# One-bank score tiles, half-width exponentials and a new order of TensorE's steps in a fused attention and gated-MLP block

## The chip, the cores and the metric

The kernel runs on one core of one Trainium2 chip. The metric is device time in microseconds (us), taken as the median of several executions. One further execution was recorded by the hardware profiler; durations and waits quoted below come from that execution.

## What is computed

The block has 2048 positions of width 512. Its first half is attention with 32 heads of 16 channels, its second a gated MLP that mixes positions. Cut to what matters:

```python
def _A_ref(x, wqkv, wo):
    H = 32; Dh = D // H                       # 16
    qkv = ...(x @ wqkv).reshape(B, S, 3, H, Dh)...
    scores = jnp.einsum("bhqd,bhkd->bhqk", q, k) * Dh ** -0.5
    p = _softmax(scores, axis=-1)
    o = jnp.einsum("bhqk,bhkd->bhqd", p, v)
    return ...o... @ wo
...
h = x + _A_ref(_layernorm(x), A_wqkv, A_wo)
h2 = h + _B_ref(_layernorm(h), B_w_in, B_w_sp, B_b_sp, B_w_out)
```

The change touches only the attention loop, and one line of the stage ahead of it.

## The kernel before, in words

The program has four stages: projections (to about 162 us of the span), the attention loop (to about 1331 us), the first part of the MLP, and the second. Around the change, each engine has its instructions in the order in which the code emits them (`manual_schedule`), and waits at the first one that is not ready.

**The attention loop** works on groups of four heads (`hg`) and blocks of 512 queries (`qb`). A *unit* is one block of 128 keys (`kb`) for four heads and 512 queries. One **iteration** of the loop takes two units, `kb` and `kb1`; there are 256 iterations, eight for each `hg`, `qb`. In an iteration:

- `score` (L777 to L789) makes the scores of two heads, the pair number `p` of a unit. Head `t` = 0 has its operands in rows 0 to 49 of TensorE's array and head `t` = 1 in rows 64 to 113 (`RG` is 64), and products of different `t` start side by side in the trace. Each product fills 512 columns, which is one PSUM bank. A tile `s` holds both products, that is two banks; there are two such tiles (`ps_s`, `bufs=2`). One ScalarE exponential of 1024 columns (L788) moves the tile to `pt` in SBUF.
- `weigh` (L791 to L797), called **the weighing** here, multiplies the four `pt` halves of one unit by V and adds them into the tile `pv` over sixteen units. It is done one unit late: the first weighing of an iteration is that of the previous iteration's `kb1`, the second that of `kb`. At the first iteration of each eight, `gather` (L799) copies the finished `pv` out, half on VectorE (L802) and half on ScalarE (L803); three iterations later `invert` takes a reciprocal of the sums on VectorE.
- `max_pair` (L205 to L253) makes, eleven calls ahead of need, the row maxima that the exponentials subtract. It returns eight **steps**, each a product of 128 queries with 512 keys into one of three one-bank tiles `m0`, `m1`, `m2`, and what reads that bank. Four steps (`four`) belong to `t` = 1. For `t` = 0, two steps take keys 1024 to 2047; and the keys below 1024 are replaced by the sums and differences of its two halves: `minus` is the product with the differences, of which ScalarE takes the absolute value (L233, called **Abs** here), and `plus` the product with the sums, where one VectorE instruction (L237) adds Abs to it and takes the maximum, since max(a, b) = (a + b)/2 + |a - b|/2. The other six steps end in one VectorE maximum each (L228). At the end of every eighth call VectorE reduces all maxima (L243), GpSimd splits them in two, and in the next iteration VectorE transposes them (`max_rows`, L255), from where SyncE's DMAs bring them beside the queries.

PSUM has eight banks: three for `m`, four for `s`, one for `pv`. The last eleven iterations have no steps left; the `m` banks are closed there, and a third tile `s` and a bank `h` take their place. GpSimd meanwhile prepares weights for the MLP, in portions that are handed out per iteration.

The steps are called one by one with a bank number written into the code, `steps.pop(0)(b)`. The emission order of one iteration before is: the scores of `kb` (`p` 0, then 1), `four[0]` (bank 2), keys 1024 to 1535 (bank 0), the first weighing, `minus` (bank 1), the copies of `gather` if due, `four[1]` (bank 2), scores of `kb1` `p` 0, `four[2]` (bank 0), scores of `kb1` `p` 1, `four[3]` (bank 1), `plus` (bank 2), the second weighing, `max_rows` if due, keys 1536 to 2047 (bank 1).

In the projection stage `ahead` (L532) lays the steps of the first eleven calls between projection products, on five banks in turn, in an order of its own.

Of the kernel before, what the change touches and what calls it, by code (L numbers as in the profile page):

```python
# [8 lines left out]
F32 = mybir.dt.float32  # L9
# [4 lines left out]
AF = mybir.ActivationFunctionType  # L14
ALU = mybir.AluOpType
AX = mybir.AxisListType
PSUM = bass.MemoryType.PSUM
DRAM = bass.MemoryType.DRAM

P = 128  # L20
# [7 lines left out]
NB = S // P  # L28
HB = NB // 2
NQ = S // 512  # L30
# [4 lines left out]
KM = 50  # L35
PB = 6
FIRST = 2
RG = 64
# [20 lines left out]
def block_kernel(ctx: ExitStack, tc: tile.TileContext, x, wqkv, wo, w_in, w_sp4, b_sp, w_out, out):  # L59
# [7 lines left out]
    nc = tc.nc  # L67
# [76 lines left out]
    kst = [kpool.tile([RG + KM, 2, S], F16, name="kst0")]  # L144
    uvs = [kpool.tile([KS, 2, 1024], F16, name="uvs0")]
    qst, mx, turned = {}, {}, {}
# [58 lines left out]
    def max_pair(m):  # L205

        g, i = divmod(m, 8)
        hg, qb = divmod(g, NQ)
        q, k, w = qst[g], kst[hg % 2], uvs[hg % 2]
        if i == 0:
            mx[g] = sm.tile([P, 16, 4], F32, name="mx")
            nc.gpsimd.memset(mx[g][:, :8, 3:], LOW)
        c, p = slice(i % 4 * P, i % 4 * P + P), i // 4
        at = lambda t, e: mx[g][:, t * 8 + i, e:e + 1]

        def scores(t, keys, b):  # L220
            r = slice(RG * t, RG * t + KS)
            acc = bank(b)
            nc.tensor.matmul(acc, q[r, p, c], keys[r, p], start=True, stop=True)  # L223
            return acc

        def one(t, e, b):
            acc = scores(t, k[:, :, 512 * e:512 * e + 512], b)
            nc.vector.reduce_max(at(t, e if t else e - 1), acc, axis=AX.X)  # L228

        def minus(b):  # L230
            acc = scores(0, w[:, :, 512:], b)
            ab[0] = sm.tile([P, 512], F32, name="ab")
            nc.scalar.activation(ab[0], acc, AF.Abs)  # L233

        def plus(b):
            acc = scores(0, w[:, :, :512], b)
            nc.vector.tensor_tensor_reduce(ab[0], acc, ab[0], 0.5, LOW, ALU.add, ALU.max, at(0, 0))  # L237

        def last(b):
            one(0, 3, b)  # L240
            if i == 7:
                nm = sm.tile([P, 2, 8], F32, name="nm")
                nc.vector.tensor_reduce(nm.rearrange("p t i -> p (t i)"), mx.pop(g), axis=AX.X,  # L243
                                        op=ALU.max, negate=True)
                parts = sm.tile([P, 2, 2, 8], F16, name="mparts")
                nc.gpsimd.tensor_scalar(nm, nm, 1.0 / ONE, 1.0, op0=ALU.mult, op1=ALU.mult)  # L246
                nc.gpsimd.tensor_copy(parts[:, :, 0], nm)
                nc.gpsimd.tensor_sub(parts[:, :, 1], nm, parts[:, :, 0])
                turned[0] = (g, parts)

        ab = {}
        four = [lambda b, e=e: one(1, e, b) for e in range(4)]
        return [four[0], lambda b: one(0, 2, b), minus, four[1], four[2], four[3], plus, last]  # L253

    def max_rows():  # L255

# [12 lines left out]
    with ExitStack() as pre:  # L269
        p2 = pre.enter_context(tc.tile_pool(name="pre_2", bufs=2))  # L270
        pc = pre.enter_context(tc.tile_pool(name="pre_c", bufs=1))
        pt = pre.enter_context(tc.tile_pool(name="pre_pt", bufs=2, space=PSUM))
# [257 lines left out]
        todo, done = [], [0]  # L530

        def ahead(k):  # L532
            for _ in range(k):
                m = done[0] // 8
                if not todo and m < LEAD:
                    steps = max_pair(m)
                    todo.extend(steps[i] for i in (0, 1, 3, 2, 4, 6, 5, 7))
                if todo:
                    todo.pop(0)(done[0] % 5)
                    done[0] += 1  # L540
# [67 lines left out]
        for g in range(3):  # L608
            a, b = 4 * g, 4 * g + 4
# [123 lines left out]
    def make_h(sb, acc):  # L733

        o2, h = o2s.pop(sb), xrs[sb]
        for d in range(DB):
            mm3(acc, o2[0][:, d, :], o2[1][:, d, :], wo2[0][:, d, :], wo2[1][:, d, :],
                d == 0, d == DB - 1)
        nc.vector.scalar_tensor_tensor(h, acc, h_down, h, op0=ALU.mult, op1=ALU.add)
        nc.sync.dma_start(h_scr[sb * P:(sb + 1) * P, :], h)  # L740
        hst[sb] = e2.tile([P, 6], F32, name="st")
        nc.vector.bn_stats(hst[sb], h)
# [24 lines left out]
    with ExitStack() as at:  # L767
# [2 lines left out]
        uvs.append(kpool1.tile([KS, 2, 1024], F16, name="uvs1"))  # L770
        fixed(kst[1])
        pp = at.enter_context(tc.tile_pool(name="pp", bufs=6))
        ps_s = at.enter_context(tc.tile_pool(name="ps_s", bufs=2, space=PSUM))
        ps_v = at.enter_context(tc.tile_pool(name="ps_v", bufs=1, space=PSUM))
        pv = {}

        def score(hg, qb, kb, p):  # L777

            q, k = qst[hg * NQ + qb], kst[hg % 2]
            turn[0] += len(later)  # L780
            pool = later[0] if turn[0] % 3 == 2 else ps_s
            s = pool.tile([P, 2, 512], F32, name="s")
            for t in range(2):
                r = slice(RG * t, RG * t + KM)
                nc.tensor.matmul(s[:, t, :], k[r, p, kb * P:(kb + 1) * P], q[r, p, :],  # L785
                                 start=True, stop=True)
            t = pp.tile([P, 2, 512], F32, name="pt")
            nc.scalar.activation(t, s, AF.Exp, scale=scales_[hg // 2])  # L788
            return t  # L789

        def weigh(hg, qb, kb, pts):  # L791
            if kb == 0:
                pv[0] = ps_v.tile([P, 512], F32, name="pv")
            for j in range(4):
                c = (4 * kb + j) * VW
                nc.tensor.matmul(pv[0][32 * j:32 * j + 32, :], vst[hg % 2][:, c:c + 32],  # L796
                                 pts[j % 2][:, j // 2, :], start=kb == 0, stop=kb == NB - 1)  # L797

        def gather(hg, qb, pool=sm):  # L799

# [39 lines left out]
        pool = nc.gpsimd  # L840
# [176 lines left out]
                quarters(p, c)  # L1017

        units = [(hg, qb, kb) for hg in range(HG) for qb in range(NQ) for kb in range(NB)]
        prev, turn, later, asked = None, [0], [], []  # L1020
        for n in range(0, len(units), 2):
            (hg, qb, kb), (_, _, kb1) = units[n:n + 2]
            if m % 8 < 7 and n < 480:
                work(4.1 if m % 8 < 6 else 2.0)
            if n == 480:
                work(None)
            if hg + 1 < HG and n % 64 < 24 and n % 4 == 0:
                load_k(hg + 1, [n % 64 // 4])
            if hg + 1 < HG and n % 64 < 12 and n % 4 == 2:
                load_uv(hg + 1, [n % 64 // 4])  # L1030
            if hg + 1 < HG and n % 64 == 30:
                copy_v = load_v(hg + 1)
            if hg + 1 < HG and n % 64 == 36:
                copy_v()
            if kb == 2 and n // NB + 3 < HG * NQ:
                load_q(n // NB + 3)
            steps = max_pair(m) if m < 8 * HG * NQ else []
            m += 1
            if not steps and not later:
                maxima.close()  # L1040
                later.append(attn.enter_context(
                    tc.tile_pool(name="ps_l", bufs=1, space=PSUM, side="right")))
            step = lambda b: steps and steps.pop(0)(b)
            pts = [score(hg, qb, kb, 0), score(hg, qb, kb, 1)]
            step(2)
            step(0)
            if prev is None:

                pv[0] = ps_v.tile([P, 512], F32, name="pv")
                for j in range(4):  # L1050
                    nc.tensor.matmul(pv[0][32 * j:32 * j + 32, :], vst[0][:, :32],
                                     vst[0][:, :512], start=True, stop=True)
            else:
                weigh(*prev)
            step(1)
            if kb == 0 and n:
                gather(*units[n - 1][:2])
            step(2)
            pts1 = [score(hg, qb, kb1, 0)]
            step(0)  # L1060
            pts1.append(score(hg, qb, kb1, 1))
            step(1)
            step(2)
            weigh(hg, qb, kb, pts)
            if turned:
                max_rows()
            step(1)
            prev = (hg, qb, kb1, pts1)
            if kb == 6 and n > NB:
                invert()  # L1070
            if n in (486, 490, 506):
                asked.append(load_o(h_rows[min((n - 486) // 4, 2)]))
            if n in (492, 496, 508):
                asked.pop(0)()
            if n in (494, 502):
                split_o(h_rows[(n - 494) // 8])
            if n in (500, 504):
                sb = h_rows[(n - 500) // 4]
                make_h(sb, later[0].tile([P, 512], F32, name="h"))
                mv, rs = scale_h(sb)  # L1080
                hns[sb] = e2.tile([P, D], F32, name="hn", bufs=3)
                nc.vector.tensor_scalar(hns[sb], xrs.pop(sb), mv[:, 0:1], rs,
                                        op0=ALU.subtract, op1=ALU.mult)
# [305 lines left out]
```

## Time and profile before

| what | us |
|---|---|
| median of 3 runs | 1777.41 |
| their range | 1774.44 to 1777.6 |
| the profiled execution | 1775.32 |
| its span, first to last instruction | 1773.2 |
| TensorE busy in the span | 1736.3 |
| VectorE busy | 1407.9 |
| ScalarE busy | 1271.0 |
| GpSimd busy | 824.3 |

The profile names engines PE (TensorE's products), PEld (its weight loads), DVE (VectorE), ACT (ScalarE), POOL (GpSimd), SP (SyncE). A timeline row gives the start, the time from the start of the first to the end of the last instruction in the row, the engine, the line, what is written and read, and a count; idle time of the engine ahead of it and what ended it stand in brackets. Products overlap in TensorE's pipeline, so the distance between the starts of two rows tells more than the rows' own lengths. The granted TensorE clock was 0.999 over the span.

### The profile page before, as it was taken

How to read it: one execution, taken by the hardware profiler on the slowest of the kernel's cores; microseconds unless marked ns; L12 is line 12 of the kernel's file. 1: busy time of each engine (PE TensorE's matmuls, PEld its weight loads, DVE VectorE, ACT ScalarE, POOL GpSimd, SP SyncE). 2: the span in 40 equal slices, each digit the busy share in tenths (PEclk: the TensorE clock that was granted, in tenths of full speed). 3: DMA queues.
4: the chain of work that ended last, by engine and by line, in shares of the span. 5: the costliest groups of instructions: out<-in, count | busy, mean ns of one | idle time of the engine just before them, and what ended most of it. 6: DMA issues, size and time to landing. Idle time of an engine off the chain costs nothing.

```text
span 1773.2 us, 32918 instructions
## 1 busy us (share of the span) xinstructions
PE 1736.3 (98%) x11621; PEld 661.6 (37%) x11621; DVE 1407.9 (79%) x2896; ACT 1271.0 (72%) x1614; POOL 824.3 (46%) x1088
## 2 busy tenths in 40 slices
PE   9999999999999999999999999999998999999999
PEld 4433222222222222222222222222225666777776
DVE  7688999999999999999999999999925886111112
ACT  4335999999999999999999999999984555011000
POOL 1322677765762168776677757700002775110010
PEclk9999999999999999999999999999999999999999
DMA  5534332232221235435344434300024463753450
GB/s 178 158 102 145 82 83 84 79 91 69 74 62 20 57 110 145 127 112 138 95 123 128 126 102 136 95 21 10 12 65 115 134 184 110 270 195 129 151 184 25
DMA packets 188029, 191.72 MB, mean 108 GB/s; under 512 B 70568, under 2 KB 139240, under 8 KB 187864
## 3 DMA queue, kind: packets, MB, share of 16 engines
q1 hardware_dynamic: 185560, 183.99, 35.8%
q10 hardware_dynamic: 2304, 5.64, 0.8%
q8 instruction: 91, 1.49, 0.4%
q14 instruction: 74, 0.61, 0.1%
HBM read 124.66 MB, written 64.56 MB: 107 GB/s over the span
## 4 chain that ended last, share of the span: by engine, by line
PE 62%; ACT 18%; issue 9%; DVE 7%; POOL 2%; DMA 2%; SPq 0%; ACTq 0%; POOLq 0%; DVEq 0%
PE pv L796 17%; PE m L223 13%; ACT pt L788 11%; PE s L785 6%; ACT ab L233 5%; PE acc L107 4%; PE acc L109 4%; PE acc L108 4%; PE g L107 4%; PE g L108 4%; PE g L109 4%; DVE rs_t L124 1%; DVE mx L228 1%; DVE rs_u L126 1%; ACT z L1148 1%
## 5 line engine op out<-in xcount | busy, mean ns | idle before, releaser
L788 ACT ACTIVATE pt<-s 128x1024 f32<-128x1024 f32 x1024 | 996.2, 1038 | 75.7 <-PE s L785 72.2
L228 DVE TENSOR_REDUCE mx<-m 128x1 f32<-128x512 f32 x1511 | 963.4, 683 | 28.3 <-PE m L223 10.5
L796 PE MATMUL pv<-pt,vst 128*32 128x512 f32 x4096 | 551.9, 605 | 0.8 <-ACT og L803 0.8
L223 PE MATMUL m<-kst,qst 48*128 48x512 f16 x1511 | 479.6, 379 | 18.8
L785 PE MATMUL s<-qst,kst 50*128 50x512 f16 x2048 | 426.5, 379 | 2.3 <-DVE mx L228 0.6
L223 PEld LDWEIGHTS <-qst 48*128 48x128 f16 x2048 | 149.6, 94 | 541.5 <-issue 505.0
L785 PEld LDWEIGHTS <-kst 50*128 50x128 f16 x2048 | 141.1, 94 | 155.2 <-issue 79.7
L246 POOL TENSOR_SCALAR nm<-nm 128x16 f32<-128x16 f32 x32 | 6.5, 204 | 403.5 <-DVE nm L243 381.4
L223 PE MATMUL m<-uvs,qst 48*128 48x512 f16 x503 | 191.8, 381 | 0.0
L237 DVE CUSTOM_DVE_ANT_0 ab<-m,ab 128x512 f32<-128x512 f32 x252 | 171.1, 679 | 0.4 <-PE m L223 0.4
L233 ACT ACTIVATE ab<-m 128x512 f32<-128x512 f32 x251 | 151.5, 604 | 18.9 <-PE m L223 18.8
L796 PEld LDWEIGHTS pv<-pt,vst 128*32 128x32 f32 x4096 | 82.9, 108 | 178.0 <-issue 161.5
L1258 ACT ACTIVATE pT<-tp 128x384 fp32r<-128x384 f32 x32 | 14.0, 488 | 142.0 <-PE tp L1250 142.0
L1336 POOL TENSOR_TENSOR pr<-pr,z 128x344 f32<-128x344 f32 x8 | 7.3, 910 | 193.1 <-DVE pr L1335 193.1
L965 POOL TENSOR_TENSOR op<-raw,op 128x512 f16<-128x512 f32 x80 | 92.7, 1159 | 5.8
L872 POOL TENSOR_TENSOR raw<-raw 128x512 f32<-128x512 f32 (+1 forms) x84 | 83.1, 989 | 6.2
L877 POOL TENSOR_TENSOR acc_sp<-acc_sp,raw 128x512 f32<-128x512 f32 x63 | 80.3, 1275 | 4.5
L1280 DVE TENSOR_TENSOR y<-acc,h 128x512 f32<-128x512 f32 x16 | 11.1, 691 | 85.9 <-PE acc L1276 84.5
L107 PE MATMUL acc<-wi,hT 128*128 128x344 f16 x256 | 79.1, 309 | 0.0
L108 PE MATMUL acc<-wi,hT 128*128 128x344 f16 x256 | 79.1, 309 | 0.0
L109 PE MATMUL acc<-wi,hT 128*128 128x344 f16 x256 | 79.1, 309 | 0.0
L725 POOL TENSOR_TENSOR o<-o,rc 128x512 f32<-128x512 f32 x16 | 20.3, 1269 | 96.3 <-DMA rc<-r_scr 68.2
(233 smaller groups left out, 2297.8 us busy)
## 6 DMA issues: line engine op xcount, KB each, us to landing
raw<-in_w_sp SPq DMA_DIRECT2D x128, 256.0 KB
s_scr<-op SPq DMA_DIRECT2D x64, 256.0 KB
op<-s_scr SPq DMA_DIRECT2D x32, 512.0 KB
a_scr<-op SPq DMA_DIRECT2D x48, 256.0 KB
op<-a_scr SPq DMA_DIRECT2D x24, 512.0 KB
qst<-q_scr SPq DMA_DIRECT2D x192, 32.0 KB
kst<-k_scr SPq DMA_DIRECT2D x48, 128.0 KB
raw<-in_w_in SPq DMA_DIRECT2D x32, 172.0 KB
```

What stands on the lines that cost most here:

```text
L107: nc.tensor.matmul(ps, lh, rh, start=first, stop=False, **kw)
L108: nc.tensor.matmul(ps, lh, rl, start=False, stop=False, **kw)
L109: nc.tensor.matmul(ps, ll, rh, start=False, stop=last, **kw)
L223: nc.tensor.matmul(acc, q[r, p, c], keys[r, p], start=True, stop=True)
L228: nc.vector.reduce_max(at(t, e if t else e - 1), acc, axis=AX.X)
L233: nc.scalar.activation(ab[0], acc, AF.Abs)
L237: nc.vector.tensor_tensor_reduce(ab[0], acc, ab[0], 0.5, LOW, ALU.add, ALU.max, at(0, 0))
L785: nc.tensor.matmul(s[:, t, :], k[r, p, kb * P:(kb + 1) * P], q[r, p, :], start=True, stop=True)
L788: nc.scalar.activation(t, s, AF.Exp, scale=scales_[hg // 2])
L796: nc.tensor.matmul(pv[0][32 * j:32 * j + 32, :], vst[hg % 2][:, c:c + 32], pts[j % 2][:, j // 2, :], start=kb == 0, stop=kb == NB - 1)
L872: pool.tensor_mul(got[0] if n else acc, got[0], got[0])
L965: chores.append((lambda: pool.tensor_sub(t[0][:, 1], of(), t[0][:, 0]), TT))
```

## The change

There are four edits, all in the attention part.

1. **Tiles.** `ps_s` holds four tiles `s` of one bank instead of two of two banks. `score` is now called for each `t` by itself, makes one product, and one exponential of 512 columns into its half of `pt`. The loop's last part has two more one-bank tiles in place of one two-bank tile.
2. **Order.** The emission order of one iteration is now: score `kb` `p` 0 `t` 0, `four[0]`, keys 1024 to 1535, score `kb` `p` 0 `t` 1, scores `kb` `p` 1 (`t` 0, 1), keys 1536 to 2047, the first weighing, the copies of `gather` if due, `minus`, `four[1]`, scores `kb1` `p` 0 (`t` 0, 1) and `p` 1 `t` 0, `four[2]`, `max_rows` if due, score `kb1` `p` 1 `t` 1, `plus`, `four[3]`, the second weighing.
3. **Banks of the steps.** The number written into the code is replaced by a running count modulo three.
4. **The list of steps.** The second step of `t` = 0 comes earlier and `four[3]` is the last; `ahead` permutes the new list so that `plus` follows `minus` directly.

The number of products, of maxima and of weighings is unchanged; ScalarE has 2048 exponentials of 512 columns instead of 1024 of 1024.

On TensorE, this is the piece of an iteration from the last scores to the second weighing. The names are tile and instance; `m1_8329` is an instance of bank `m1`. Before, from the scores of `kb1`, `p` 1:

```order
L785 LDWEIGHTS kst1_1855
L785 MATMUL s_8324<-qst_6546,kst1_1855 128x512 [waits Activation_49]
L785 LDWEIGHTS kst1_1855
L785 MATMUL s_8324<-qst_6546,kst1_1855 128x512
L223 LDWEIGHTS qst_7543
L223 MATMUL m1_8329<-kst1_1855,qst_7543 128x512 [waits Activation_49]
L223 LDWEIGHTS qst_7543
L223 MATMUL m2_8332<-uvs1_1856,qst_7543 128x512 [waits DVE_49]
L796 MATMUL pv_8018<-pt_8292,vst1_163 32x512
L796 MATMUL pv_8018<-pt_8297,vst1_163 32x512
L796 MATMUL pv_8018<-pt_8292,vst1_163 32x512
L796 MATMUL pv_8018<-pt_8297,vst1_163 32x512
```

And the same place in the changed kernel, from its last score half on:

```order
L786 LDWEIGHTS kst1_1855
L786 MATMUL s_10141<-qst_8255,kst1_1855 128x512 [waits Activation_49]
L223 LDWEIGHTS qst_8807
L223 MATMUL m0_10144<-uvs1_1856,qst_8807 128x512 [waits Activation_49]
L223 LDWEIGHTS qst_8807
L223 MATMUL m1_10147<-kst1_1855,qst_8807 128x512 [waits DVE_49]
L795 MATMUL pv_9995<-pt_10093,vst1_163 32x512
L795 MATMUL pv_9995<-pt_10106,vst1_163 32x512
L795 MATMUL pv_9995<-pt_10093,vst1_163 32x512
L795 MATMUL pv_9995<-pt_10106,vst1_163 32x512
```

Before, the two steps ahead of the weighing are `four[3]`, which waits for Abs (its bank is that of `minus`), and `plus`, which waits for the maximum of `four[1]`. Now they are `plus`, which waits for Abs, and `four[3]`, which waits for the maximum of `four[1]`; every score half has a wait of its own.

On ScalarE, one iteration before has four exponentials and one Abs:

```order
L788 ACTIVATE pt_9300<-s_9297 128x1024 [waits PE_49,Activation_49]
L788 ACTIVATE pt_9305<-s_9302 128x1024 [waits PE_49,Activation_49]
L233 ACTIVATE ab_9319<-m1_9317 128x512 [waits PE_49]
L788 ACTIVATE pt_9327<-s_9324 128x1024 [waits PE_49,Activation_49]
L788 ACTIVATE pt_9335<-s_9332 128x1024 [waits PE_49,Activation_49]
```

In the changed kernel it has eight exponentials of half the width, with Abs again in the middle:

```order
L788 ACTIVATE pt_8113<-s_8114 128x512 [waits PE_49]
L788 ACTIVATE pt_8113<-s_8123 128x512 [waits PE_49]
L788 ACTIVATE pt_8126<-s_8127 128x512 [waits PE_49]
L788 ACTIVATE pt_8126<-s_8130 128x512 [waits PE_49]
L233 ACTIVATE ab_8142<-m0_8140 128x512 [waits PE_49]
L788 ACTIVATE pt_8147<-s_8148 128x512 [waits PE_49]
L788 ACTIVATE pt_8147<-s_8151 128x512 [waits PE_49]
L788 ACTIVATE pt_8154<-s_8155 128x512 [waits PE_49]
L788 ACTIVATE pt_8154<-s_8161 128x512 [waits PE_49]
```

Two halves share one tile `pt` and have a tile `s` each.

The diff, cut to its core:

```diff
         def last(b):
-            one(0, 3, b)
+            one(1, 3, b)
...
         four = [lambda b, e=e: one(1, e, b) for e in range(4)]
-        return [four[0], lambda b: one(0, 2, b), minus, four[1], four[2], four[3], plus, last]
+        two = [lambda b, e=e: one(0, e, b) for e in (2, 3)]
+        return [four[0], two[0], two[1], minus, four[1], four[2], plus, last]
...
-                    todo.extend(steps[i] for i in (0, 1, 3, 2, 4, 6, 5, 7))
+                    todo.extend(steps[i] for i in (0, 1, 4, 2, 5, 3, 6, 7))
...
-        ps_s = at.enter_context(tc.tile_pool(name="ps_s", bufs=2, space=PSUM))
+        ps_s = at.enter_context(tc.tile_pool(name="ps_s", bufs=4, space=PSUM))
...
+        def score(hg, qb, kb, p, t):
+
+            if not t:
+                pts[p, kb] = pp.tile([P, 2, 512], F32, name="pt")
+            turn[0] += 1
+            pool = later[0] if later and turn[0] % 6 > 3 else ps_s
+            s = pool.tile([P, 512], F32, name="s")
+            r = slice(RG * t, RG * t + KM)
+            nc.tensor.matmul(s, kst[hg % 2][r, p, kb * P:(kb + 1) * P],
+                             qst[hg * NQ + qb][r, p, :], start=True, stop=True)
+            nc.scalar.activation(pts[p, kb][:, t, :], s, AF.Exp, scale=scales_[hg // 2])
...
-                    tc.tile_pool(name="ps_l", bufs=1, space=PSUM, side="right")))
-            step = lambda b: steps and steps.pop(0)(b)
-            pts = [score(hg, qb, kb, 0), score(hg, qb, kb, 1)]
-            step(2)
-            step(0)
+                    tc.tile_pool(name="ps_l", bufs=2, space=PSUM, side="right")))
+
+            def step():
+                if steps:
+                    steps.pop(0)(count[0] % 3)
+                    count[0] += 1
+
+            both = lambda k, p, *ts: [score(hg, qb, k, p, t) for t in ts]
+            both(kb, 0, 0)
+            step()
+            step()
+            both(kb, 0, 1)
+            both(kb, 1, 0, 1)
+            step()
...
-            step(1)
             if kb == 0 and n:
                 gather(*units[n - 1][:2])
-            step(2)
-            pts1 = [score(hg, qb, kb1, 0)]
-            step(0)
-            pts1.append(score(hg, qb, kb1, 1))
-            step(1)
-            step(2)
-            weigh(hg, qb, kb, pts)
+            step()
+            step()
+            both(kb1, 0, 0, 1)
+            both(kb1, 1, 0)
+            step()
             if turned:
                 max_rows()
-            step(1)
-            prev = (hg, qb, kb1, pts1)
+            both(kb1, 1, 1)
+            step()
+            step()
+            weigh(hg, qb, kb)
+            prev = (hg, qb, kb1)
```

More of the change, by code (lines that the diff above doesn't have):

```diff
@@ L772, in block_kernel, with weigh @@
         pp = at.enter_context(tc.tile_pool(name="pp", bufs=6))
-        ps_s = at.enter_context(tc.tile_pool(name="ps_s", bufs=2, space=PSUM))
+        ps_s = at.enter_context(tc.tile_pool(name="ps_s", bufs=4, space=PSUM))
         ps_v = at.enter_context(tc.tile_pool(name="ps_v", bufs=1, space=PSUM))
         pv = {}
[L777 to L791, printed above, removed]
+        def score(hg, qb, kb, p, t):
[8 more added lines that the diff above has]
+            nc.scalar.activation(pts[p, kb][:, t, :], s, AF.Exp, scale=scales_[hg // 2])
+        def weigh(hg, qb, kb):
             if kb == 0:
@@ L796, in weigh @@
                 nc.tensor.matmul(pv[0][32 * j:32 * j + 32, :], vst[hg % 2][:, c:c + 32],
-                                 pts[j % 2][:, j // 2, :], start=kb == 0, stop=kb == NB - 1)
+                                 pts[j % 2, kb][:, j // 2, :], start=kb == 0, stop=kb == NB - 1)
+            for p in range(2):
+                del pts[p, kb]
         def gather(hg, qb, pool=sm):
@@ L1019, in block_kernel @@
         units = [(hg, qb, kb) for hg in range(HG) for qb in range(NQ) for kb in range(NB)]
-        prev, turn, later, asked = None, [0], [], []
+        prev, turn, count, later, asked, pts = None, [0], [0], [], [], {}
         for n in range(0, len(units), 2):
@@ L1078, in block_kernel @@
                 sb = h_rows[(n - 500) // 4]
-                make_h(sb, later[0].tile([P, 512], F32, name="h"))
+                make_h(sb, later[0].tile([P, 512], F32, name="h", bufs=1))
                 mv, rs = scale_h(sb)
```

## The prediction

> **What bounds the kernel now.** I read the page first, then the stages, then one iteration of the attention loop on three engines. From the page, the span, the engines' line, and the costliest group on each of ScalarE and VectorE:
>
> ```profile
> span 1773.2 us, 32918 instructions
> PE 1736.3 (98%) x11621; PEld 661.6 (37%) x11621; DVE 1407.9 (79%) x2896; ACT 1271.0 (72%) x1614; POOL 824.3 (46%) x1088
> L788 ACT ACTIVATE pt<-s 128x1024 f32<-128x1024 f32 x1024 | 996.2, 1038 | 75.7 <-PE s L785 72.2
> L228 DVE TENSOR_REDUCE mx<-m 128x1 f32<-128x512 f32 x1511 | 963.4, 683 | 28.3 <-PE m L223 10.5
> ```
>
> The table by stretch (PE, PEld, DVE, ACT, POOL busy) has one row in the projections and one in the loop; the third row below is Abs, once per iteration with steps:
>
> ```profile
> 130.00:162.00 32.00, 32.00 (x161) 11.87 (x159) 27.40 (x51) 10.28 (x19) 3.91 (x8) 1.00 0.38 115
> 600.00:1280.00 680.00, 667.63 (x4751) 175.65 (x4748) 664.85 (x1262) 638.80 (x762) 388.93 (x505) 1.00 0.35 98
> ...
> L233 ACT ACTIVATE ab<-m x245: 597/605/607, 164.4 to 1282.5; 128x512 f32<-128x512 f32 x123
> ```
>
> In the loop three engines look 94 to 98% busy, so shares don't name the limit. Abs gives the pace: 244 distances in 1282.5 - 164.4 = 1118.1 us, **4.58 us per iteration**, 36.66 per eight. The limit is read from one iteration, first TensorE:
>
> ```profile
> 910.91 0.39 PE L223 MATMUL m<-uvs,qst 48*128 48x512 f16 x1
> 910.91 0.39 PE L223 MATMUL m<-kst,qst 48*128 48x512 f16 x1
> 911.14 0.38 PE L785 MATMUL s<-qst,kst 50*128 50x512 f16 x2
> 911.36 0.38 PE L223 MATMUL m<-kst,qst 48*128 48x512 f16 x1
> 911.57 0.39 PE L785 MATMUL s<-qst,kst 50*128 50x512 f16 x2
> 912.06 0.37 PE L223 MATMUL m<-kst,qst 48*128 48x512 f16 x1
> 912.11 0.37 PE L223 MATMUL m<-uvs,qst 48*128 48x512 f16 x1
> 912.42 1.06 PE L796 MATMUL pv<-pt,vst 128*32 128x512 f32 x8
> 913.41 0.39 PE L223 MATMUL m<-kst,qst 48*128 48x512 f16 x1
> 913.42 0.86 PE L785 MATMUL s<-qst,kst 50*128 50x512 f16 x4
> 914.10 0.40 PE L223 MATMUL m<-kst,qst 48*128 48x512 f16 x2
> 914.43 1.06 PE L796 MATMUL pv<-pt,vst 128*32 128x512 f32 x8
> 915.43 0.39 PE L223 MATMUL m<-uvs,qst 48*128 48x512 f16 x1
> ```
>
> then VectorE's maximum of `four[1]`, the second product of the next tile `s`, and ScalarE with the exponential that waits for it:
>
> ```profile
> 911.37 0.69 DVE L228 TENSOR_REDUCE mx<-m 128x1 f32<-128x512 f32 x1
> ...
> 913.64 0.64 PE L785 MATMUL s<-qst,kst 50*128 50x512 f16 x3
> ...
> 911.40 0.60 ACT L233 ACTIVATE ab<-m 128x512 f32<-128x512 f32 x1
> 911.88 1.96 ACT L788 ACTIVATE pt<-s 128x1024 f32<-128x1024 f32 x2
> 914.13 1.94 ACT L788 ACTIVATE pt<-s 128x1024 f32<-128x1024 f32 x2 [0.29 <-PE s L785]
> ```
>
> `minus` and `four[1]` start together at 910.91, each with a wait of its own: a pair of different rows costs one slot, 911.14 - 910.91 = 0.23. A weighing holds TensorE 1.00 (914.43 to 915.43) and begins 0.31 after the last step (912.11 to 912.42). Abs ends at 912.00 and `four[3]` starts at 912.06; the maximum of `four[1]` ends at 912.06 and `plus` starts at 912.11. So TensorE waits about half a microsecond there while no engine is the culprit. The iteration is **a ring**: `minus`/`four[1]` to second weighing 1.51, weighing 0.99, scores and two steps 1.02, first weighing 1.00; sum 4.52. The 36.66 per eight is 8 x 4.52 = 36.16, and 0.50 of extras: copies, reciprocal, transposes.
>
> **The change part by part.** *Second half of the ring.* Three banks and eight steps mean that a step reuses the bank of the third step before it. `plus` therefore still waits for Abs, and `four[3]`, now last, for the maximum of `four[1]`. The same chain as now: product to VectorE 0.46 (910.91 to 911.37), 0.69, restart 0.05, 0.31 to the weighing: 1.51. By way of Abs: product to ScalarE 0.49 (913.64 to 914.13), 0.60, restart 0.06, 0.31: 1.46, just beneath. The rotation removes no wait here; 1.51 stays.
>
> *First half.* Now three pairs and a lone step: three slots of 0.225 and 0.31, that is 0.99 in place of 1.02. Each score half needs the bank of the half four places earlier. Follow them from Abs on: the halves of `kb1` start 0.48, 0.96, 1.43 and 1.91 after Abs, the last ends at 2.51, that is 3.00 after `minus`; the scores of the next `kb` start 1.51 + 1.00 = 2.51 after `minus`, their fourth half would be due at 2.96, and so is the only one to be late, by 0.1, on rows that the lone step doesn't use. So the ring is 1.51 + 1.00 + 0.99 + 1.00 = **4.50**.
>
> *Halves on ScalarE.* No exponential of 512 columns is in the trace. The nearest row is Abs, same width, types and memories: the next instruction starts 911.88 - 911.40 = 0.48 later. Two full exponentials start 0.90 apart (1.96 less about 1.06). The ends: not under 0.45 (half of 0.90), not over 0.60, Abs's own duration, if nothing overlapped. I take 0.48. An iteration then needs 9 x 0.48 = 4.32 of ScalarE, 4.08 before. The cover is the ring, 4.50: 0.18 of slack; without it the halves cost 0.24 per iteration.
>
> The Trainium skill speaks against this edit: ScalarE: Activation LUTs, What ACT_TABLE_LOAD costs, gives 186 ns + 0.833 per column with 93 ns overlapped, by estimate 0.52 per half, 4.68 per iteration and 1807 in the end (the second rival below). The row of Abs with its 0.48 contradicts it here. By the Trainium skill, Perfetto Trace Analysis, Optimizing Scalar/DVE Operations, the overhead from PSUM is about 51 ns, by estimate 0.48, as the row has it.
>
> *Extras.* At `gather`, one in eight:
>
> ```profile
> 603.65 0.39 PE L223 MATMUL m<-uvs,qst 48*128 48x512 f16 x1
> 605.36 0.64 PE L796 MATMUL pv<-pt,vst 128*32 128x512 f32 x4
> ...
> 603.99 0.41 DVE L802 COPY og<-pv 128x256 f32<-128x256 f32 x1
> 604.32 1.28 DVE L228 TENSOR_REDUCE mx<-m 128x1 f32<-128x512 f32 x2
> ...
> 604.68 0.41 ACT L803 ACTIVATE og<-pv 128x256 f32<-128x256 f32 x1
> 604.94 1.06 ACT L788 ACTIVATE pt<-s 128x1024 f32<-128x1024 f32 x1
> ```
>
> VectorE's copy holds `four[1]` up by 0.33 less its slack, so `minus` to weighing was 605.36 - 603.65 = 1.71, 0.20 over 1.51. It stays there. ScalarE's copy now stands ahead of Abs instead of behind it, 0.26 (604.68 to 604.94); VectorE's delay runs beside it, so I add 0.19 in all. The other extras on VectorE:
>
> ```profile
> 914.45 0.24 DVE L760 RECIPROCAL rcp<-sums 128x16 f32<-128x16 f32 x1
> 914.61 1.22 DVE L228 TENSOR_REDUCE mx<-m 128x1 f32<-128x512 f32 x2
> ...
> 809.19 0.22 DVE L243 TENSOR_REDUCE nm<-mx 128x16 f32<-128x64 f32 x1
> 809.33 3.07 DVE L228 TENSOR_REDUCE mx<-m 128x1 f32<-128x512 f32 x5
> ```
>
> They take 0.16 and 0.14, the transpose about as much. VectorE has seven passes of 0.60 ((3.07 - 0.69) / 4), 4.2 in 4.50, and 0.3 to absorb one of them; they fall into three different iterations. Now each is felt in part (0.50 less 0.20 for three of them and for catching up after `gather`); I leave a third of that, 0.10 per eight, since the score halves no longer wait for a whole two-bank tile. Together 8 x 4.50 + 0.19 + 0.10 = 36.29, a gain of 0.37 per eight, and 245 / 8 = 30.6 eights: **-11.3 us**.
>
> *The last eleven iterations* have no ring through the steps; ScalarE runs without a break:
>
> ```profile
> 1287.36 9.27 ACT L788 ACTIVATE pt<-s 128x1024 f32<-128x1024 f32 x10 [0.24 <-PE s L785]
> ```
>
> That is about 0.905 each; two halves are 0.96, and 44 of them cost **+2.4**. Six one-bank tiles are as deep as three of two.
>
> *The rest, nothing.* Before the loop TensorE is busy 32.00 of 32.00 us, VectorE 27.40: `plus` behind `minus` there may make VectorE wait for Abs about 0.05 each time, eleven times, 0.5 in all if VectorE had no slack. `max_rows` keeps its SyncE transfers and gets a little more time after the maxima. The number of TensorE's products is the same.
>
> Sum: 1775.3 - 11.3 + 2.4 = 1766.4 for an execution like the profiled one; the median of the runs is 2.1 above it, so **1768.5**.
>
> **The rivals.** *Extras fall on the ring.* Now `four[0]` and the next step stand between score halves, so a maximum that is 0.14 to 0.33 late holds back exponentials as well. For: VectorE is 98% busy. Against: 0.3 of slack in 4.50. All of 0.33 + 0.16 + 0.14 + 0.13 on the ring: 36.76 per eight, +3.1, and +2.4: 1783.
>
> *ScalarE becomes the ring: slower.* Place: eight halves and Abs. It decides from 4.58 / 9 = 0.51 per instruction. For: nothing shows two half exponentials in a row. Against: Abs's 0.48. With a third of the 0.12 overlap lost, 0.52: 4.68, +0.10 x 245 = 24, and the end +6: 1807. With all of it lost, 0.60: 5.40, +201, and the end +13: 1991, which the 0.48 all but excludes.
>
> *The change doesn't shorten the first half.* If the late fourth half delays the weighing by its 0.1 after all in some iterations, the ring returns to 4.52 to 4.55 and the tail's 2.4 comes on top: 1777.
>
> *The slack swallows all extras and the slot is shorter.* If the first half takes 0.93 and only `gather` is left: 8 x 4.44 + 0.19 = 35.7, -29 and +2.4: 1751.
>
> **How the numbers follow.** Forecast 1768, own range 1759 to 1776: 0.46. Extras on the ring, 1776 to 1788: 0.24. ScalarE, 1790 and up: 0.10. No shortening, 1774 to 1781: 0.08. Better, 1747 to 1759: 0.12. A measurement of this kernel can tell about 0.2%, 3.6 us, so the borders are 1773.9 and 1781.0. Faster: 0.44 of the forecast's and all 0.12, 0.56. Same: 0.02, a quarter of the second case (0.06) and 0.08, 0.16. Slower: 0.18 + 0.10, 0.28. The range takes in everything but ScalarE's case and the outer edges: 1748 to 1789.
>
> **What would show it.** Right: Abs 4.54 us apart on average and 4.50 in plain iterations; `four[3]` starting 0.05 after the end of the maximum of `four[1]`, and the weighing 1.51 after `minus`; half exponentials 0.48 apart with idle time in every iteration. Wrong: no idle time on ScalarE (its ring decides), a wait of `four[0]` or the lone step for VectorE in plain iterations, or pairs that no longer start together, each 0.23 dearer.

## The result and the profile after

| what | before | changed |
|---|---|---|
| median, us | 1777.41 (1774.44 to 1777.6, 5 runs) | 1768.62 (1767.67 to 1769.73, 5 runs) |
| ratio, with 95% interval | | 0.9955 (0.9940 to 0.9969) |
| span of the profiled execution | 1773.2 | 1765.9 |

The change makes the kernel 0.45% faster; the forecast was 1768. From the page of the changed kernel, two of the lines that answer to those of before:

```profile
PE 1725.2 (98%) x11621; PEld 643.5 (36%) x11621; DVE 1395.1 (79%) x2896; ACT 1324.2 (75%) x2638; POOL 825.8 (47%) x1088
L788 ACT ACTIVATE pt<-s 128x512 f32<-128x512 f32 x2048 | 1042.9, 620 | 7.9 <-PE s L786 5.0
```

ScalarE's exponentials are busy 47 us longer (1042.9 against 996.2) and its waits for scores fell from 72.2 to 5.0; both are nearly invisible in the total. What counts is the pace. Abs in the changed kernel, once per iteration with steps:

```profile
L233 ACT ACTIVATE ab<-m x245: 591/597/648, 164.5 to 1272.4; 128x512 f32<-128x512 f32 x123
```

1272.4 - 164.5 = 1107.9 us for 244 distances, 4.54 each, where it was 1118.1 and 4.58: **10.2 us less in the loop**. From the last Abs to the end of the span it is 493.5 against 490.7, **2.8 more**. The last product of the last weighing starts at 1326.1 in the changed kernel and at 1333.0 before, so the last eleven iterations take 53.7 against 50.5, 3.2 more, and the MLP behind them 0.4 less. No run changes the MLP, and its time differs by 3 us between the eight traces (439.6 to 442.7), so the 0.4 says nothing. The start is unmoved (164.4 and 164.5).

A plain iteration, that is one without `gather` and the other extras, TensorE first. The score halves and the steps mix, so the timeline puts several in one row:

```profile
904.03 0.39 PE L223 MATMUL m<-uvs,qst 48*128 48x512 f16 x1
904.04 0.39 PE L223 MATMUL m<-kst,qst 48*128 48x512 f16 x1
904.26 0.59 PE L786 MATMUL s<-qst,kst 50*128 50x512 f16 x3
...
905.10 0.37 PE L223 MATMUL m<-uvs,qst 48*128 48x512 f16 x1
905.23 0.37 PE L223 MATMUL m<-kst,qst 48*128 48x512 f16 x1
905.54 1.06 PE L795 MATMUL pv<-pt,vst 128*32 128x512 f32 x8
906.53 0.39 PE L786 MATMUL s<-qst,kst 50*128 50x512 f16 x1
...
907.20 0.38 PE L223 MATMUL m<-kst,qst 48*128 48x512 f16 x1
907.50 1.07 PE L795 MATMUL pv<-pt,vst 128*32 128x512 f32 x8
908.50 0.39 PE L223 MATMUL m<-uvs,qst 48*128 48x512 f16 x1
```

then the maximum of `four[1]` on VectorE, and ScalarE:

```profile
904.49 0.69 DVE L228 TENSOR_REDUCE mx<-m 128x1 f32<-128x512 f32 x1
...
904.46 0.60 ACT L233 ACTIVATE ab<-m 128x512 f32<-128x512 f32 x1
904.95 4.07 ACT L788 ACTIVATE pt<-s 128x512 f32<-128x512 f32 x8
908.93 0.60 ACT L233 ACTIVATE ab<-m 128x512 f32<-128x512 f32 x1
```

The ring reads 1.51 (904.03 to 905.54), 0.99, 0.97, 1.00: 4.47. Abs ends at 905.05 and `plus` starts at 905.10; the maximum of `four[1]` ends at 905.18 and `four[3]` starts at 905.23; the weighing follows 0.31 later. TensorE still waits for both.

Over a stretch of the loop (PE, PEld, DVE, ACT, POOL busy) ScalarE now looks the busiest of all:

```profile
600.00:1270.00 670.00, 654.23 (x4721) 163.80 (x4715) 653.62 (x1255) 665.40 (x1348) 385.86 (x500) 1.00 0.35 99
```

The prediction had named missing idle time on ScalarE as a sign that its ring decides, and by this row the sign is there, 665.40 of 670.00 us busy. It misleads: a busy instruction counts to its end, which overlaps the next one. By the distance of starts, 0.478 us (worked out below), eight halves and Abs need 4.30 of the 4.47, and the kernel without `four[3]` below has the same nine at a pace of 4.41.

The iteration with `gather` is the dear one. VectorE's copy, ScalarE's copy and Abs, then TensorE:

```profile
890.42 0.41 DVE L803 COPY og<-pv 128x256 f32<-128x256 f32 x1
...
890.87 0.38 ACT L804 ACTIVATE og<-pv 128x256 f32<-128x256 f32 x1 [0.22 <-DVE og L803]
891.15 0.59 ACT L233 ACTIVATE ab<-m 128x512 f32<-128x512 f32 x1
...
890.13 0.39 PE L223 MATMUL m<-uvs,qst 48*128 48x512 f16 x1
...
891.79 0.37 PE L223 MATMUL m<-uvs,qst 48*128 48x512 f16 x1 [0.62 <-ACT ab L233]
892.12 0.64 PE L795 MATMUL pv<-pt,vst 128*32 128x512 f32 x4
```

`minus` (890.13) to weighing takes 1.99 here, 0.48 more than in the plain iteration, and `plus` waits 0.62 for Abs. ScalarE's copy did not start until VectorE's had ended (890.42 + 0.41 = 890.83), and Abs stood behind it.

### The profile page after: what moved, and what is told of

Its sections match the earlier page's. It is cut to its first block, busy times and chain, and to the rows that moved or that the text cites. A ratio compares the mean times of both kernels' runs of the same rounds, so it can differ in the third digit from the quotient of the medians.

```text
span 1765.9 us, 32751 instructions
## 1 busy us (share of the span) xinstructions
PE 1725.2 (98%) x11621; PEld 643.5 (36%) x11621; DVE 1395.1 (79%) x2896; ACT 1324.2 (75%) x2638; POOL 825.8 (47%) x1088
## 4 chain that ended last, share of the span: by engine, by line
PE 69%; DVE 14%; ACT 11%; DMA 2%; issue 2%; POOL 2%; SPq 1%; DVEq 0%; ACTq 0%; POOLq 0%
PE pv L795 20%; PE m L223 12%; PE s L786 11%; ACT pt L788 7%; DVE mx L228 7%; PE acc L107 4%; PE acc L109 4%; PE acc L108 4%; PE g L107 4%; PE g L108 4%; PE g L109 4%; ACT ab L233 2%; DVE ab L237 1%; DVE rs_t L124 1%; DVE rs_u L126 1%
## 5 line engine op out<-in xcount | busy, mean ns | idle before, releaser
L788 ACT ACTIVATE pt<-s 128x512 f32<-128x512 f32 x2048 | 1042.9, 620 | 7.9 <-PE s L786 5.0
L223 PE MATMUL m<-kst,qst 48*128 48x512 f16 x1510 | 527.6, 379 | 0.1
L786 PE MATMUL s<-qst,kst 50*128 50x512 f16 x2048 | 443.0, 377 | 0.4 <-DVE mx L228 0.4
L223 PEld LDWEIGHTS <-qst 48*128 48x128 f16 x2048 | 143.7, 93 | 389.0 <-issue 376.5
L786 PEld LDWEIGHTS <-kst 50*128 50x128 f16 x2048 | 125.4, 95 | 315.9 <-issue 229.3
```

The source lines that it names most:

```text
L786: nc.tensor.matmul(s, kst[hg % 2][r, p, kb * P:(kb + 1) * P], qst[hg * NQ + qb][r, p, :], start=True, stop=True)
L788: nc.scalar.activation(pts[p, kb][:, t, :], s, AF.Exp, scale=scales_[hg // 2])
```

## The experiments

The theory: the loop's pace is a ring through TensorE, in which the second weighing stands behind two steps that wait for Abs and for the maximum of `four[1]`; half tiles shorten what the scores wait for only in an order that spreads them; `gather` costs because it delays Abs. Rivals stand in the expectations. Each kernel was measured against the kernel before on the same chip, whose medians there were 1776.88 us for the first four and 1776.67 for the last two.

### The copy behind Abs

```diff
-            if kb == 0 and n:
-                gather(*units[n - 1][:2])
-            step()
             step()
+            if kb == 0 and n:
+                gather(*units[n - 1][:2])
+            step()
```

> The changed kernel with one line moved: gather is emitted after the step minus instead of ahead of it, so ScalarE takes Abs before its half of the copy of pv. Theory (ring, and the copy on ScalarE waits for VectorE's copy and so holds Abs back): the iteration with gather and the one after it, 5.07 + 4.35 = 9.42 us in the changed kernel, fall to about 4.70 + 4.47 = 9.17; with 0.25 to 0.28 in each of 31 places 8 us less, about 1761 us. Rival (VectorE's copy ahead of the maximum of four[1] is what costs): nothing moves, 1768 to 1769.

Measured: 1759.97 us, ratio 0.9904 (0.9891 to 0.9918). The same place in its trace, VectorE's copy, ScalarE and TensorE:

```profile
884.79 0.41 DVE L803 COPY og<-pv 128x256 f32<-128x256 f32 x1
...
884.92 0.60 ACT L233 ACTIVATE ab<-m 128x512 f32<-128x512 f32 x1
885.42 0.38 ACT L804 ACTIVATE og<-pv 128x256 f32<-128x256 f32 x1
...
884.50 0.39 PE L223 MATMUL m<-uvs,qst 48*128 48x512 f16 x1
...
885.57 0.37 PE L223 MATMUL m<-uvs,qst 48*128 48x512 f16 x1
885.86 0.37 PE L223 MATMUL m<-kst,qst 48*128 48x512 f16 x1
886.16 0.64 PE L795 MATMUL pv<-pt,vst 128*32 128x512 f32 x4
```

Abs starts 0.42 after `minus` instead of 1.02, and `minus` to weighing takes 1.66 instead of 1.99. What remains over the plain 1.51 is VectorE's copy ahead of the maximum of `four[1]` (`four[3]` is last, at 885.86). The theory holds, with 0.33 gained at each place where it had 0.25 to 0.28, and this kernel is faster than the kernel before and the changed one.

### Halves in the old order

```diff
-        ps_s = at.enter_context(tc.tile_pool(name="ps_s", bufs=2, space=PSUM))
+        ps_s = at.enter_context(tc.tile_pool(name="ps_s", bufs=4, space=PSUM))
...
-            s = pool.tile([P, 2, 512], F32, name="s")
             for t in range(2):
...
+                s = pool.tile([P, 512], F32, name="s")
...
+                nc.scalar.activation(pt[:, t, :], s, AF.Exp, scale=scales_[hg // 2])
-            nc.scalar.activation(t, s, AF.Exp, scale=scales_[hg // 2])
```

This is the kernel before, with the steps and banks as they were.

> The kernel before with only the tiles changed: four one-bank tiles and half exponentials, the old order of steps and the old bank numbers. Theory (ring): in the old order four scores stand side by side right after a weighing and the fourth waits for the end of the fourth half after Abs; Abs start to that end 2.56, one pair of steps 0.22, 0.31 to the weighing, 1.00 of weighing, 0.49 to the next Abs: 4.59, and with the ends of back-to-back halves sliding, 4.64 to 4.69 per iteration against 4.58: 15 to 27 us more and 2.8 in the last eleven iterations, 1795 to 1805 us. Rival (the halves bring the gain by themselves): at most 1770.

Measured: 1796.84 us, ratio 1.0112 (1.0097 to 1.0128), slower as the theory had it. Abs over the whole loop:

```profile
L233 ACT ACTIVATE ab<-m x245: 597/632/633, 164.2 to 1299.5; 128x512 f32<-128x512 f32 x123
```

and its timeline over two iterations, ScalarE, then TensorE, with VectorE's maximum of `four[1]`:

```profile
897.47 2.06 ACT L788 ACTIVATE pt<-s 128x512 f32<-128x512 f32 x4 [0.17 <-PE s L786]
899.39 0.63 ACT L233 ACTIVATE ab<-m 128x512 f32<-128x512 f32 x1
...
901.30 0.69 ACT L788 ACTIVATE pt<-s 128x512 f32<-128x512 f32 x1
...
903.98 0.61 ACT L233 ACTIVATE ab<-m 128x512 f32<-128x512 f32 x1
...
896.83 0.39 PE L223 MATMUL m<-kst,qst 48*128 48x512 f16 x1
...
902.04 0.37 PE L786 MATMUL s<-qst,kst 50*128 50x512 f16 x1
...
902.56 1.06 PE L796 MATMUL pv<-pt,vst 128*32 128x512 f32 x8
903.56 0.39 PE L223 MATMUL m<-uvs,qst 48*128 48x512 f16 x1
...
904.01 0.69 DVE L228 TENSOR_REDUCE mx<-m 128x1 f32<-128x512 f32 x1
...
904.76 0.37 PE L223 MATMUL m<-uvs,qst 48*128 48x512 f16 x1
905.06 0.64 PE L796 MATMUL pv<-pt,vst 128*32 128x512 f32 x4
```

4.65 per iteration (1135.3 / 244), inside the expectation. But the path that the expectation named is only half of it: plain iterations take 4.59 and 4.64 in turn, and the trace shows two paths that take turns.

- *4.59, the path of the expectation.* From Abs at 899.39 the fourth half after it ends 2.60 later (901.30 + 0.69 = 901.99), the fourth score starts 0.05 behind that end (902.04), the weighing at 902.56, `minus` at 903.56, and the next Abs 0.42 after it, at 903.98.
- *4.64, by way of VectorE and ScalarE.* From `minus` at 903.56 the maximum of `four[1]` ends at 904.70, `plus` starts at 904.76 and the second weighing at 905.06, 1.50 after `minus`. A weighing takes 1.00; then come the last step and the first score, 0.64 from that step to the first half exponential (in the iteration before: 896.83 to 897.47), and four halves, 1.92 (897.47 to 899.39). 905.06 + 1.00 + 0.64 + 1.92 = 908.62 is the next Abs, 4.64 behind 903.98. An Abs of this kind waits for the halves ahead of it and not for its product: at 899.39 it is 0.52 behind `minus` (898.87), where 0.42 would do.

So in the old order the four halves lie on the path in every second iteration, 1.92 where two full exponentials took 1.82 (905.06 to 906.88 in the trace of before).

### The new order with whole tiles

```diff
-        ps_s = at.enter_context(tc.tile_pool(name="ps_s", bufs=4, space=PSUM))
+        ps_s = at.enter_context(tc.tile_pool(name="ps_s", bufs=2, space=PSUM))
...
+                full[0] = pool.tile([P, 2, 512], F32, name="s")
...
-            nc.scalar.activation(pts[p, kb][:, t, :], s, AF.Exp, scale=scales_[hg // 2])
+            if t:
+                nc.scalar.activation(pts[p, kb], full[0], AF.Exp, scale=scales_[hg // 2])
```

This is the changed kernel with a two-bank tile taken at `t` = 0.

> The changed kernel with the old tiles: two two-bank tiles and exponentials of 1024 columns, the new order of steps and the rotating banks. Theory: the new order needs the halves; with whole tiles the first score after a weighing still waits for a whole exponential, and ScalarE starts only when both products are there: 4.51 to 4.56 in plain iterations, gather as dear as in the changed kernel, 4.59 on average against 4.54, without the 2.8 at the end: 1775 to 1781 us, no gain over the kernel before. Rival (the order brings the gain by itself): 1763 to 1766, since the dearer end is saved.

Measured: 1781.02 us, ratio 1.0020 (1.0011 to 1.0029): no gain, a small loss, at the upper edge of the expectation. Abs over the whole loop:

```profile
L233 ACT ACTIVATE ab<-m x245: 592/605/607, 164.8 to 1288.3; 128x512 f32<-128x512 f32 x123
```

and ScalarE's timeline in one iteration:

```profile
894.99 1.94 ACT L789 ACTIVATE pt<-s 128x1024 f32<-128x1024 f32 x2 [0.28 <-PE s L786]
```

4.60 per iteration, 4.54 in plain ones. ScalarE idles 0.28 after the weighing, until both products of the tile are there, as in the kernel before (0.29).

So each part alone loses, 1.12% and 0.20%, and together they gain 0.45%. In the changed kernel ScalarE starts on the first score half behind the weighing instead of waiting for a pair, and its halves lie off the ring.

### Bank numbers fixed again

```diff
+            count[0] = 0
+
             def step():
```

> The changed kernel with the count of banks set to zero at each iteration, so that each step always has the same bank (0, 1, 2, 0, 1, 2, 0, 1). Theory: the second and third step of an iteration then reuse banks that were filled two or three steps earlier, keys 1024 to 1535 the bank of four[3]; it waits for that maximum 0.28 longer than in the changed kernel, and score halves stand behind it: 4.76 to 4.81 per iteration against 4.54, 55 to 66 us more, 1822 to 1835 us. Rival (rotation is only tidier): 1767 to 1771.

Measured: 1830.83 us, ratio 1.0302 (1.0286 to 1.0317). Abs over the whole loop, then the maximum of `four[3]` and TensorE behind the weighing:

```profile
L233 ACT ACTIVATE ab<-m x245: 592/597/598, 164.4 to 1333.7; 128x512 f32<-128x512 f32 x123
...
904.24 0.69 DVE L228 TENSOR_REDUCE mx<-m 128x1 f32<-128x512 f32 x1
...
904.47 0.87 PE L223 MATMUL m<-kst,qst 48*128 48x512 f16 x2
904.98 0.60 PE L786 MATMUL s<-qst,kst 50*128 50x512 f16 x3
```

That maximum ends at 904.93. The step for keys 1024 to 1535, the second product of the row from 904.47, would be due one slot of 0.23 later, at 904.70. It starts together with the score half behind it, at 904.98, 0.28 late. The pace is 4.79 on average (1169.3 / 244) against 4.54, and time and pace lie inside the expectation. Rotation is needed by the new order.

### Without `four[3]`

```diff
-            nc.gpsimd.memset(mx[g][:, :8, 3:], LOW)
+            nc.gpsimd.memset(mx[g][:, :, 3:], LOW)
...
-            one(1, 3, b)
             if i == 7:
...
-                    count[0] += 1
+                    count[0] += bool(steps)
```

The empty slot of the maxima is filled with a low number, and the count of banks leaves out the step that has no product any more.

> The changed kernel without the product and the maximum of four[3] in all 256 calls: keys 1536 to 2047 of the heads t = 1 are left out of the maxima, so the exponentials subtract a number that may be too small. One of seven VectorE passes and one of eight steps of TensorE go. Theory (ring): the second weighing then waits for plus alone, and plus for Abs; 0.49 + 0.60 + 0.05 + 0.31 = 1.45 instead of 1.50, so plain iterations go from 4.47 to 4.43 and no further, about 10 us less in the loop, 1757 to 1760 us. Rival (the loop runs at the pace of VectorE, which looks 98% busy): a pass of 0.60 less in each of 245 iterations, down to ScalarE's 4.30, 40 us less or more, at most 1730.

Measured: 1752.33 us, ratio 0.9862 (0.9845 to 0.9878). TensorE, ScalarE, VectorE:

```profile
902.04 0.39 PE L223 MATMUL m<-uvs,qst 48*128 48x512 f16 x1
...
903.17 0.37 PE L223 MATMUL m<-uvs,qst 48*128 48x512 f16 x1
903.47 0.64 PE L794 MATMUL pv<-pt,vst 128*32 128x512 f32 x4
...
902.46 0.66 ACT L233 ACTIVATE ab<-m 128x512 f32<-128x512 f32 x1
...
904.93 0.69 DVE L228 TENSOR_REDUCE mx<-m 128x1 f32<-128x512 f32 x1 [0.45 <-PE m L223]
```

VectorE now idles 0.45 at that point, and a seventh of its passes is gone; the pace hardly follows. VectorE as the bound is refuted. The weighing waits for Abs alone, 1.43 after `minus`, and the plain iteration is 4.41. The gain over the changed kernel is 16 us (in the loop 1091.7 against 1107.9), outside the expectation, which had 10. Two of its terms are off and in part cancel: product to Abs is 0.42, not 0.49, and Abs itself takes 0.66, not 0.60. What is left is 0.02 per iteration, 5 us.

### The transpose behind `four[3]`

```diff
-            if turned:
-                max_rows()
+            late_rows = bool(turned)
             both(kb1, 1, 1)
             step()
             step()
             weigh(hg, qb, kb)
+            if late_rows:
+                max_rows()
```

This stands on the kernel with the copy behind Abs.

> The kernel with gather after minus, and besides max_rows after the second weighing, so that VectorE's transpose stands behind the maximum of four[3] instead of ahead of the instruction for plus. Theory: the transposing iteration of each eight, 4.52 in the changed kernel, falls to the plain 4.47, 30 times 0.05, 1.5 us less than with gather alone: 1758 to 1759 us. Rival (the extra 0.05 comes from elsewhere, such as the transfers of max_rows): 1760.

Measured: 1759.73 us, ratio 0.9907 (0.9891 to 0.9924); against 1759.97 it can't be told apart, and the total doesn't decide. The trace does: the dearer iteration is still there with the transpose moved. VectorE and TensorE at the place:

```profile
905.55 0.22 DVE L243 TENSOR_REDUCE nm<-mx 128x16 f32<-128x64 f32 x1
905.68 1.88 DVE L228 TENSOR_REDUCE mx<-m 128x1 f32<-128x512 f32 x3
...
906.96 0.39 PE L223 MATMUL m<-uvs,qst 48*128 48x512 f16 x1
907.02 0.37 PE L223 MATMUL m<-kst,qst 48*128 48x512 f16 x1
```

My theory of the 0.05 falls. `four[1]` starts 0.06 after `minus` here, where the two start together elsewhere: it reuses the bank of keys 1024 to 1535, whose maximum was put off by the reduction of all maxima ahead of it. That the reduction is the cause is read from these rows; no kernel was run that moves it. One more trace agrees: the kernel without `four[3]` keeps the reduction and has one VectorE pass less, and there this iteration takes 4.41, like the plain ones.

## Why the prediction was right, step by step

- **Where the limit was read.** Right: no engine's share, but a ring with the second weighing behind two waits. `no_last` and `banks_fixed` show it, by taking one wait away and by adding one. Of the signs named, the pace (4.54), the 0.05 ahead of `four[3]` and the 1.51 came true; idle time on ScalarE in every iteration does not show in the listing, as said above.
- **Second half of the ring, 1.51.** Right to the hundredth (904.03 to 905.54), with VectorE's chain behind `four[3]` last. Abs's chain was put just beneath; it is 0.07 shorter than I had it, since a product reaches Abs in 0.42. My 0.49 came from a full exponential, which in the program waits for two semaphores where Abs and the halves wait for one. That this makes the 0.07 is argued, not shown.
- **First half, 0.99.** Measured 0.97 (906.53 to 907.50). With smaller remainders in the other parts the ring is 4.47, not 4.50: 0.03 x 245 = 7 us more gain than forecast.
- **Halves at 0.48.** Right. The last eleven iterations have rows without a break; here is one of 24 halves, then its last half alone:

```profile
1275.46 11.87 ACT L788 ACTIVATE pt<-s 128x512 f32<-128x512 f32 x24 [0.51 <-PE s L786]
...
1286.46 0.87 ACT L788 ACTIVATE pt<-s 128x512 f32<-128x512 f32 x1
```

  With 0.87 for the last one, (11.87 - 0.87) / 23 = 0.478. The cost at the end was forecast at 2.4 and is 3.2 up to the last weighing; 44 x (2 x 0.478 - 0.905) gives 2.2 of it, and where the rest comes from stays open. ScalarE did not become the ring: without `four[3]` the loop runs at 4.41 with the same halves. By the figures of the Trainium skill, ScalarE: Activation LUTs, What ACT_TABLE_LOAD costs, a half would take about 0.52 by estimate; this row has 0.478, so the measurement decides against it for this shape out of PSUM. The page's figure is for an immediate scale, and here the scale comes from a register.
- **`gather`, +0.19.** Wrong: 0.48, in 31 places 9 us less gain. The step that failed is "VectorE's delay runs beside it". ScalarE's copy waited for VectorE's copy of the same tile, so the two delays lie behind one another, and Abs behind both. In the program that copy carries a wait for VectorE; I had priced it by its length alone (and by the rows that I showed, 1.71 - 1.51 or 1.46 + 0.26 - 1.51, the term should have been 0.20 or 0.21, not 0.19). `gather_later`, in which Abs stands ahead of ScalarE's copy and the rest keeps its order, shows that the greater part came by Abs: 0.33 of the 0.48 went. The remaining 0.15 is VectorE's copy ahead of the maximum of `four[1]`.
- **Other extras, 0.10 per eight.** Measured 0.05, from the reduction, as far as the rows tell; reciprocal and transpose are absorbed.
- **The sum.** 8 x 4.47 + 0.48 + 0.05 = 36.3 per eight, forecast 36.29. That the time came out to a microsecond is luck, errors that cancel: the ring 7 us too long, the small extras 1.5 too long, `gather` 9 too short. The split of the gain was wrong, too. Of the 0.37 per eight the forecast had 0.16 from a shorter ring (36.16 to 36.00) and 0.21 from cheaper extras (0.50 to 0.29). In the trace the ring gives all of it (36.16 to 35.8), and the extras cost as much as before, 0.53.
- **The rivals.** Extras on the ring: only `gather` did, by another route. Not shortening, and ScalarE as the ring: did not occur in this order; the old order with halves is the case in which ScalarE's halves lie on the path, in every second iteration.

## What to carry to other kernels

Where three engines look 95% busy, follow one iteration from a wait to its releaser until the path closes, and price a change by what it does to that closed path, not by busy time: here a seventh of VectorE's passes was worth 0.06 of 4.47 us. Read the slack of an engine from the starts of its instructions, since busy time counts ends that overlap. Finer tiles and a new order can each lose alone and gain together, as here, so try them together. Before an instruction is moved ahead of another on the same engine, look up what it waits for: a copy that waits for another engine's copy brings that wait along.

## What the runs showed of the hardware that was not expected

In an unbroken row of half exponentials the starts keep a distance of 0.478 us while each lasts longer than the one before: in the row of 24 above, the first takes 0.60 us and the last 0.87, and the mean in the changed kernel is 620 ns. So the work keeps its pace while the ends come later and later.

Who waits for the end of such an instruction waits longer the longer ScalarE has run without a break. The trace of the old order with halves shows it: the half at 901.30 takes 0.69, and the score that waits for its bank starts at 902.04, 0.05 behind that later end.
